# Attention, a dense MLP and routed experts in one kernel: an instruction planner that counts transfer bytes, the second batch's logits taken at once, and sums moved from TensorE to VectorE

## The chip, the cores and the metric

The kernel runs on one core of one Trainium2 chip. The metric is device time in microseconds (us); less is better. A kernel is timed in several executions, of which the median counts, and one further execution is recorded by the profiler.

## The reference, cut to what matters

```python
# q, k, v: (4 batches, 12 heads, 448, 64); w_in 768x2048, w_out 2048x768; w1 8x768x1024, w2 8x1024x768
scores = 30 * tanh((q @ k.T) / 8 / 30);  attn = softmax(scores);  x = attn @ v      # tokens 1792 x 768
h = x @ w_in;  g = h * clip(h + 3, 0, 6) / 6;  x = g @ w_out                        # dense MLP
logits = x @ w_gate                                                                 # 1792 x 8
# greedy: the largest logits first, each token to one expert, 224 tokens for each expert
out[tokens of e] = relu(x[tokens of e] @ w1[e]) @ w2[e]
```

All matrices are fp32. The dense weights come as float64 and are turned into fp32 words by integer operations on VectorE.

## The kernel before

**Three stages.** The first (to about 505 us) does attention for the four batches, the product x @ w_in with its activation g, and the logits. The second (about 505 to 797 us) does g @ w_out and, beside it, the greedy assignment in seven rounds of compares on VectorE and counts on TensorE. The third does the experts.

**The planner of the first stage.** Every step of stage one is given to `Plan.add` with an engine, a cost in us, what it reads and writes, and, for a transfer, a fixed time `land` from its issue to its landing. `Plan.run` is a list scheduler: it simulates the engines, takes at each moment the earliest step that is ready, of several the one that was added first, and emits the instructions in that order. Each engine's queue then runs in this order on the chip: an instruction that waits holds up all that stand behind it on its engine. A transfer's `land` is the same whatever else is being transferred. Names with a ring (`"ms": 1` is a single PSUM bank, `"g": 5`, `"ws": 3`, `"rb": 2`, ...) are handed on in the order of `add`.

**Attention.** A slot is half of a pair of heads (48 slots, 24 pairs, 6 pairs per batch). `score` makes two chunks of scores in PSUM, ScalarE takes tanh and exp into tiles `P`, `av` multiplies by v into `po`, and `uadd` adds the two chunks' `P` on VectorE, into `u0` for the first half of a pair and into `sb` for the second. Every second pair `fin_sum` adds over the keys: TensorE multiplies `u0` and then `sb` by ones into the bank `ms` (8 products for two pairs), VectorE makes the reciprocals `R`, SP stores them to DRAM (`rd`) and loads them back spread over the partitions (`rb`), and `fin_x` multiplies `xu` by `rb` (line 320) and splits the result into XH (a ScalarE cast, line 328, or VectorE for early pairs) and XL (line 330).

**The first product.** `m1a_pieces(b)` makes 16 column blocks f of batch b, each of 18 matmuls in three parts: wh by XH and XL for d = 0..2, the same for d = 3..5, then wl by XH for all d. Blocks f = 0, 2, 4, 6, 8 keep their split weights in SBUF (`wr`); the other 11 are split in batch 0, stored to DRAM (`wd`) and loaded again for batches 1 to 3 into the ring `ws`. From ph come r (line 540), g (line 542), and gh and gl (lines 548 and 549), which SP stores.

**Logits.** `wog_pieces` decodes w_out and multiplies it by the gate weights: transposes into `ms` (line 387), a ScalarE copy to `wot` (line 393), products (line 404). It is merged with batch 1's product. Batches 0 and 1 store g to DRAM (`gd`), and `lg_late` loads it again beside batch 2's product (line 463 multiplies). Batches 2 and 3 take their logits at once.

**Merging.** `merge` interleaves streams by their share of cost: the attention slots, the product's pieces, and what is added to them.

**The second stage.** Here the framework orders the instructions by itself. `m1b_pieces` multiplies (line 987); of w_out's blocks f = 8..15 it loads `woy`, ScalarE makes the high part `woh` (line 649), and GpSimd subtracts to the low part `wol` (line 652). The load of block f + 4 reuses a buffer of `woy` that this subtraction has read. The first eight blocks are split earlier, on ScalarE and VectorE.

Of the kernel before, what the change touches and what calls it, by code (L numbers as in the profile page):

```python
# [33 lines left out]
class Plan:  # L34
# [6 lines left out]
    HOP = 0.15  # L41

# [13 lines left out]
    def add(self, eng, cost, fn, r=(), w=(), land=0.0, after=()):  # L56
# [24 lines left out]
        deps.discard(me)  # L81
        self.ops.append((eng, cost, fn, deps, land))
        return me
# [4 lines left out]
    def run(self):  # L88
# [12 lines left out]
        total = 0.0  # L101
        for _ in range(n):
# [8 lines left out]
            _, cost, fn, _, land = self.ops[i]  # L111
            ready[eng].remove(i)
            free[eng] = t + cost
            end = t + cost + land
# [11 lines left out]
def fused_kernel(ctx: ExitStack, tc: tile.TileContext, q, k, v, cap, w_in, w_out, w_gate, w1, w2,  # L126
# [25 lines left out]
    for i in range(2):  # L152
# [7 lines left out]
    RES = [f for f in range(NF - 6) if f % 2 == 0]  # L160
# [34 lines left out]
    def load_qk(g, n):  # L195
        if g > LASTG:
            return
        b, hp = divmod(g, NP)
        key = ("t" + "kq"[n], g)
        add("SP", 0.35, lambda: nc.sync.dma_start(  # L200
            put(ap_, key, [2 * D, S]), (k, q)[n][b, 2 * hp:2 * hp + 2].rearrange("h d s -> (h d) s")), w=[key], land=2.4)

    def load_v(g):
        if g <= LASTG:
            add("SP", 0.35, lambda: nc.sync.dma_start(put(ap_, ("tv", g), [CP, 2, NC, D]), v[g // NP, g % NP]),
                w=[("tv", g)], land=2.4)
# [38 lines left out]

    def uadd(h):

        g, s_ = divmod(h, 2)
        if h < 0 or g > LASTG:
            return  # L250
        key = (("u0", "sb")[s_], g)

        def go():
            u = SB[g % 2] if s_ else put(ap_, key, [CP, 2, S])
            T[key] = u
            nc.vector.tensor_add(u[:CP], T["P", 4 * g + 2 * s_], T["P", 4 * g + 2 * s_ + 1])
        add("DVE", 1.09, go, r=[("P", 4 * g + 2 * s_), ("P", 4 * g + 2 * s_ + 1)], w=[key])
# [25 lines left out]
    def fin_sum(g):  # L283

        m, i = plan.next("ms"), g // 2

        def mm():
            p = bank(("ms", m))
            for s_ in range(2):
                for n in range(4):  # L290
                    u = T[("u0", "sb")[s_], g - 1 + n // 2]
                    r = CP + s_
                    nc.tensor.matmul(p[32 * n:32 * n + 32, :S], ones[:r], u[:r, n % 2], start=(s_ == 0), stop=(s_ == 1))  # L293
        add("PE", 1.7, mm, r=[(n, x) for n in ("u0", "sb") for x in (g - 1, g)] + [("guard", 0)], w=[("ms", m)])
# [14 lines left out]
        add("SP", 1.2, store, r=[R], w=[("RD", i)], land=2.0)  # L309
        for a in range(2):  # L310
# [4 lines left out]
            add("SP", 0.7, load, r=[("RD", i)], w=[("rb", g - 1 + a)], land=2.4)  # L315
# [32 lines left out]
    FIN = ((2, fin_sum), (4, lambda g: fin_x(g - 1)), (5, fin_x))  # L348

    def decode(src, shape, view):  # L350
# [4 lines left out]
            put(dcp, raw, shape[:-1] + [2 * shape[-1]], I32), src.bitcast(I32)), w=[raw], land=5.5)  # L355
# [14 lines left out]
    def wog_pieces():  # L370
# [3 lines left out]
        def dec(f):  # L374
            if f < NF:
                y[f] = decode(w_out[f * 128:(f + 1) * 128, :].rearrange("p (o c) -> p o c", o=1), [128, 1, DM],
                              lambda t: flat(t)[:, None, :])
                add("SP", 0.35, lambda: nc.sync.dma_start(WO[f], flat(T[y[f]])), r=[y[f]], w=[("WO", f)], land=3.0)
# [36 lines left out]
        r = [(1, lambda: (dec(0), dec(1)))]  # L415
        for f in range(NF):
            for part in range(len(PARTS)):
                r.append((300, lambda f=f, part=part: tr(f, part)))
            r.append((1, lambda f=f: dec(f + 2)))
# [12 lines left out]
    def wload(b, f):  # L432
        if f in WD:
# [6 lines left out]
            add("SP", 0.7, go, r=[("WD", f)], w=[key], land=4.0)  # L440

    def wsplit(f):
# [47 lines left out]
    def lg_late(b):  # L490
# [23 lines left out]
    def m1a_pieces(b, logits):  # L514
        gs = {}

        def mm(f, part):
# [5 lines left out]
            def go():  # L523
# [21 lines left out]
            if not logits:  # L545
                add("SP", 0.35, lambda: nc.sync.dma_start(GD[b][f], T[g]), r=[g], w=[("GD", b, f)], land=2.5)
# [31 lines left out]
    add("SP", 0.35, lambda: nc.sync.dma_start(capt, cap.to_broadcast([128, 1])), w=[("capt", 0)], land=2.0)  # L578
# [53 lines left out]
    def wo_load_p(f):  # L632
        add("SP", 0.35, lambda: wo_load(f), r=[("WO", f), ("mba", 0)], w=[("woy", f)], land=3.0)
# [556 lines left out]
```

## Time and profile before

| what | value |
|---|---|
| median of 3 runs | 1074.06 us (1073.12 to 1074.07) |
| profiled execution, its own time | 1077.6 us |
| its span, first to last instruction | 1075.6 us |
| TensorE (PE) busy | 1016.3 us, 94% |
| VectorE (DVE) busy | 732.5 us, 68% |
| ScalarE (ACT) busy | 511.1 us, 48% |
| GpSimd (POOL) busy | 150.9 us, 14% |
| bytes moved by DMA | 246.45 MB, mean 229 GB/s |

The profiled execution has 2.0 us outside its span. Busy time of PE includes matmuls that overlap, so what an idle PE costs is read from its waits and from the stretches in which it has no instruction. The granted clock is a share of 2.4 GHz: 1.00 is that level, 0.50 is 1.2 GHz.

### The profile page before, as it was taken

What the parts mean: (1) busy time and instruction counts of PE and PEld (TensorE: products, weight loads), DVE (VectorE), ACT (ScalarE), POOL (GpSimd) and SP (SyncE); (2) the same over time, 40 slices, a digit from 0 to 9 for tenths busy, and PEclk for the clock granted to TensorE, in tenths of its full rate; (3) what the DMA queues carried; (4) which work ended last, traced back from release to release, by engine and by line L of the source; (5) the groups of instructions that cost most, each with busy time, mean ns of one, the idle gap of its engine ahead of it and who ended that gap; (6) DMA issues with size and microseconds to landing.
All of it is one profiled execution on the core that took longest, in us unless ns stands there. A gap on an engine that the chain in (4) does not pass through costs nothing.

```text
span 1075.6 us, 17493 instructions
## 1 busy us (share of the span) xinstructions
PE 1016.3 (94%) x6385; PEld 829.1 (77%) x6385; DVE 732.5 (68%) x1298; ACT 511.1 (48%) x868; POOL 150.9 (14%) x154
## 2 busy tenths in 40 slices
PE   6989999699989999899899999999979999999996
PEld 2445666467666667687798899989969999999996
DVE  6898887568655444434987897778427777777673
ACT  6989877566766552433101001001116655666662
POOL 0000000000000000001500000000013555455442
PEclk8989999989999999999899999999989999999999
DMA  7467998899988669985545655537875776676760
GB/s 214 156 209 225 319 330 309 311 328 336 330 283 274 201 200 326 323 288 197 184 120 143 161 138 142 156 106 236 283 263 167 250 246 226 233 240 230 231 226 29
DMA packets 123637, 246.45 MB, mean 229 GB/s; under 512 B 23776, under 2 KB 90384, under 8 KB 123552
## 3 DMA queue, kind: packets, MB, share of 16 engines
q1 hardware_dynamic: 118960, 229.28, 64.7%
q0 software_dynamic: 3328, 11.01, 3.6%
q10 hardware_dynamic: 1264, 5.05, 1.6%
q8 instruction: 50, 0.82, 0.3%
q14 instruction: 35, 0.29, 0.1%
HBM read 182.50 MB, written 62.79 MB: 228 GB/s over the span
## 4 chain that ended last, share of the span: by engine, by line
PE 73%; DMA 12%; DVE 9%; issue 2%; ACT 2%; SPq 1%; POOL 0%; DVEq 0%; ACTq 0%; POOLq 0%
PE x L987 20%; PE py L1104 12%; PE ph L1059 7%; PE ph L533 5%; PE ph L530 5%; PE ph L531 4%; PE po L270 4%; PE ph L1061 4%; PE sc L235 3%; DMA rb<-rd 3%; PE ro L814 2%; DVE g L806 1%; PE ms L293 1%; DMA wsh<-wd 1%; DMA woy<-wo 1%
## 5 line engine op out<-in xcount | busy, mean ns | idle before, releaser
L987 PE MATMUL x<-woh,gh 128*128 128x384 f32 x448 | 127.6, 348 | 2.2 <-DMA gh<-gh 2.2
L987 PE MATMUL x<-wol,gh 128*128 128x384 f32 x448 | 124.7, 339 | 0.0
L987 PE MATMUL x<-woh,gl 128*128 128x384 f32 x448 | 123.2, 340 | 0.1
L239 ACT ACTIVATE P<-sc,rcap 112x896 f32<-112x896 f32 x96 | 92.7, 1004 | 24.1 <-PE sc L235 14.2
L530 PE MATMUL ph<-XH,wsh 128*128 128x448 f32 x264 | 99.5, 377 | 0.2 <-DVE g L542 0.2
L531 PE MATMUL ph<-XL,wsh 128*128 128x448 f32 x264 | 96.6, 366 | 0.0
L243 ACT ACTIVATE P<-P,capt 112x896 f32<-112x896 f32 x96 | 94.9, 1042 | 0.0
L270 PE MATMUL po<-P,tv 112*64 112x448 f32 x384 | 89.1, 586 | 3.4 <-ACT P L239 2.5
L987 PEld LDWEIGHTS x<-woh,gh 128*128 128x128 f32 x448 | 81.2, 191 | 9.4 <-issue 5.2
L987 PEld LDWEIGHTS x<-woh,gl 128*128 128x128 f32 x448 | 82.9, 191 | 0.7 <-DMA gl<-gl 0.4
L987 PEld LDWEIGHTS x<-wol,gh 128*128 128x128 f32 x448 | 83.2, 191 | 0.0
L540 ACT ACTIVATE r<-ph,three 128x448 f32<-128x448 f32 x64 | 40.6, 634 | 75.7 <-PE ph L533 75.7
L542 DVE SCALAR_TENSOR_TENSOR g<-r,ph 128x448 f32<-128x448 f32 x64 | 39.5, 617 | 54.1 <-ACT r L540 53.9
L806 DVE TENSOR_SCALAR g<-mrb,m 112x1344 bf16<-112x1344 f32 (+11 forms) x105 | 72.4, 701 | 0.0
L1059 PE MATMUL ph<-xe,woh 128*128 128x448 f32 x186 | 60.7, 383 | 4.5 <-DVE xe L1045 4.5
L533 PE MATMUL ph<-XH,wsl 128*128 128x448 f32 x264 | 63.4, 376 | 0.0
L530 PEld LDWEIGHTS ph<-XH,wsh 128*128 128x128 f32 x264 | 50.0, 189 | 14.3 <-issue 7.9
L722 POOL IOTA icol<- 112x112 f32 x1 | 0.2, 229 | 431.7 <-PE ph L531 431.7
L270 PEld LDWEIGHTS po<-P,tv 112*64 112x64 f32 x384 | 24.5, 144 | 46.8 <-issue 30.1
L1081 DVE SCALAR_TENSOR_TENSOR hl<-ht,hh 128x224 fp32r<-128x224 f32 x64 | 40.0, 625 | 29.3 <-ACT hh L1080 27.9
L1059 PE MATMUL ph<-xe,we 128*128 128x448 f32 x186 | 58.8, 374 | 0.0
L533 PEld LDWEIGHTS ph<-XH,wsl 128*128 128x128 f32 x264 | 49.4, 191 | 9.1 <-issue 4.4
(210 smaller groups left out, 2278.5 us busy)
## 6 DMA issues: line engine op xcount, KB each, us to landing
wol<-in_moe_w SPq DMA_DIRECT2D x32, 768.0 KB
woh<-in_moe_w SPq DMA_DIRECT2D x31, 768.0 KB
gh<-gh SPq DMA_DIRECT2D x64, 224.0 KB
gl<-gl SPq DMA_DIRECT2D x64, 224.0 KB
wsh<-wd SPq DMA_DIRECT2D x33, 384.0 KB
wsl<-wd SPq DMA_DIRECT2D x33, 384.0 KB
wraw<-in_moe_w_in SPq DMA_DIRECT2D x16, 768.0 KB
wraw<-in_moe_w_out SPq DMA_DIRECT2D x16, 768.0 KB
```

The costliest lines, as they stand in the source:

```text
L239: add("ACT", 0.96, lambda i=i: nc.scalar.activation(put(ap_, ("P", i), [CP, 2, S]), T["sc", i][:CP, :, :S], AF.Tanh, scale=rcap[:CP]), r=[ ...
L243: add("ACT", 0.99, lambda i=i: nc.scalar.activation(T["P", i], T["P", i], AF.Exp, scale=capt[:CP]), r=[("P", i), ("capt", 0)], w=[("P", i)])
L270: nc.tensor.matmul(T["po", g][64 * j:64 * j + 64, :S], T["tv", g][:, j, c, :], T["P", 4 * g + c][:, j], start=(c == 0), stop=(c == NC - 1))
L530: nc.tensor.matmul(p, wh[:, d], XH[:, d], start=(d == 0), stop=False)
L531: nc.tensor.matmul(p, wh[:, d], XL[:, d], start=False, stop=False)
L533: nc.tensor.matmul(p, wl[:, d], XH[:, d], start=False, stop=(d == KD - 1))
L540: add("ACT", 0.64, lambda: nc.scalar.activation(put(m1p, r_, [128, S]), T[key][:, :S], AF.Relu, bias=three), r=[key], w=[r_])
L806: nc.vector.tensor_scalar(g[:, s_:], mr[:, s_:], mj, None, op0=OP.is_le)
L987: nc.tensor.matmul(X2[g, i, hf][:, :HW], a, w[:, hf * HW:(hf + 1) * HW], start=bool(f == 0 and first), stop=bool(f == NF - 1 and last))
L1059: nc.tensor.matmul(p[:, :2 * TE], wh[:, d, fs], X2[:, d].rearrange("p a t -> p (a t)"), start=(d == 0), stop=False)
L1061: nc.tensor.matmul(p[:, :TE], wl[:, d, fs], X2[:, d, 0], start=False, stop=(d == KD - 1))
L1104: nc.tensor.matmul(PY[e][2 * t + hf][:CP, :384], a[:, f, tsl], w[:, f % 2, hf * 384:(hf + 1) * 384], start=bool(f == 0 and first), stop=bo ...
```

## The change

- **Planner.** A transfer now has a size `kb` in place of `land`. All transfers share one wire of 340 KB per us in order of their issue, and land 2.0 us after their last byte. The loads of `rb` are entered with 500 KB and 1.0 us of SP each (before 0.7 us of SP and 2.4 us to landing), the stores of `rd` with 8 KB, q, k, v, g, gh and gl with 224, weights with 768 or 384.
- **Weights.** Block 8 is no longer resident; the ring `g` grows from 5 to 8.
- **Sums.** For pairs 12 to 23 (batches 2 and 3) VectorE adds u0 and both chunks of the second half into `sb` (two additions in place of one), and `fin_sum` multiplies `sb` alone.
- **Order.** `fin_x` of both pairs is added one or two slots earlier; a w_out decode is added right ahead of its transposes.
- **First product.** The three parts of a block now take d = 0, 1, then 2, 3, then 4, 5, with all three products for each d, so that a part waits for two of X's blocks and not for three or all.
- **Logits.** Batches 0 and 1 are merged as one stretch; `wog_pieces` spans 37% to 89% of it. Batch 1 takes its logits at once, at blocks 6, 10 and 14 and in batch 2; its g is not stored to `gd` nor loaded again.
- **Second stage.** The subtraction to `wol` of blocks 8..15 goes from GpSimd to VectorE.

```diff
+    LAND = 2.0
+    RATE = 340.0
...
-            end = t + cost + land
+            end = t + cost
+            if kb:
+                wire = max(wire, end) + kb / self.RATE
+                end = wire + self.LAND
...
-    RES = [f for f in range(NF - 6) if f % 2 == 0]
+    RES = [f for f in range(NF - 8) if f % 2 == 0]
...
+    GB = 8
...
-                 "g": 5, "gh": 2, "gl": 2, "lacc": 1, "lacl": 1, "late": 8, "woy": 2, "gm": 4})
+                 "g": GB, "gh": 2, "gl": 2, "lacc": 1, "lacl": 1, "late": 8, "woy": 2, "gm": 4})
...
+    G3 = 12
...
-            nc.vector.tensor_add(u[:CP], T["P", 4 * g + 2 * s_], T["P", 4 * g + 2 * s_ + 1])
-        add("DVE", 1.09, go, r=[("P", 4 * g + 2 * s_), ("P", 4 * g + 2 * s_ + 1)], w=[key])
+            if s_ and g >= G3:
+                nc.vector.tensor_add(u[:CP], T["u0", g], T["P", 4 * g + 2])
+                nc.vector.tensor_add(u[:CP], u[:CP], T["P", 4 * g + 3])
+            else:
+                nc.vector.tensor_add(u[:CP], T["P", 4 * g + 2 * s_], T["P", 4 * g + 2 * s_ + 1])
+        whole = s_ and g >= G3
+        add("DVE", 2.18 if whole else 1.09, go,
+            r=[("P", 4 * g + 2 * s_), ("P", 4 * g + 2 * s_ + 1)] + [("u0", g)] * whole, w=[key])
...
+        halves = (1,) if g >= G3 else (0, 1)
...
-            for s_ in range(2):
+            for s_ in halves:
...
-        add("SP", 1.2, store, r=[R], w=[("RD", i)], land=2.0)
+        add("SP", 1.2, store, r=[R], w=[("RD", i)], kb=8)
...
-            add("SP", 0.7, load, r=[("RD", i)], w=[("rb", g - 1 + a)], land=2.4)
+            add("SP", 1.0, load, r=[("RD", i)], w=[("rb", g - 1 + a)], kb=500)
...
-    FIN = ((2, fin_sum), (4, lambda g: fin_x(g - 1)), (5, fin_x))
+    FIN = ((2, fin_sum), (3, lambda g: fin_x(g - 1)), (3, fin_x))
...
-            put(dcp, raw, shape[:-1] + [2 * shape[-1]], I32), src.bitcast(I32)), w=[raw], land=5.5)
+            put(dcp, raw, shape[:-1] + [2 * shape[-1]], I32), src.bitcast(I32)), w=[raw], kb=768)
...
-                for d in range(3 * part, 3 * part + 3) if part < 2 else ():
+                for d in range(2 * part, 2 * part + 2):
                     nc.tensor.matmul(p, wh[:, d], XH[:, d], start=(d == 0), stop=False)
                     nc.tensor.matmul(p, wh[:, d], XL[:, d], start=False, stop=False)
-                for d in range(KD) if part == 2 else ():
                     nc.tensor.matmul(p, wl[:, d], XH[:, d], start=False, stop=(d == KD - 1))
-            xs = [("X", b, n, d) for n in "hl" for d in range(3 * part, 3 * part + 3)] if part < 2 else [("X", b)]
+            xs = [("X", b, n, d) for n in "hl" for d in range(2 * part, 2 * part + 2)]
...
-                if logits and part == 1 and f % 4 == 0 and f:
+                if logits and part == 1 and f % 4 == logits - 1 and f > 3:
...
+    WO0, WO1, AP = 0.7, 0.2, 0.1
...
-    for b in range(1, B):
-        body, end = m1a_pieces(b - 1, b - 1 >= 2)
-        body.insert(int(len(body) * 0.9), (0, lambda b=b: (wload(b, 0), wload(b, 1))))
-        extra = wog_pieces() if b == 2 else lg_late(0) + lg_late(1) if b == 3 else []
-        merge(A[cut[b]:cut[b + 1]], body, extra)
-        if b == 2:
-            add("none", 0.0, turn_dec, w=[("room", 0)], after=plan.using({"wraw", "wy", "wot"}))
+    def m1a(b, logits):
+        body, end = m1a_pieces(b, logits)
+        body.insert(int(len(body) * 0.9), (0, lambda: (wload(b + 1, 0), wload(b + 1, 1))))
+        return body, end
+
+    def pad(stream, share):
+        return [(share * sum(c for c, _ in stream), lambda: None)]
+
+    body, end = m1a(1, 3)
+    extra = wog_pieces()
+    merge(A[cut[1]:cut[3]], m1a(0, 0)[0] + body, pad(extra, WO0) + extra + pad(extra, WO1))
+    add("none", 0.0, turn_dec, w=[("room", 0)], after=plan.using({"wraw", "wy", "wot"}))
+    body, end2 = m1a(2, 1)
+    body = body[:4] + end + body[4:]
+    end = end2
+    merge(A[cut[3]:] + pad(A[cut[3]:], AP), body, lg_late(0))
...
-                    wo_split(f + 2, mb, nc.gpsimd)
+                    wo_split(f + 2, mb, nc.vector)
```

## Rows read from the trace of the kernel before

**Rows 1.** Windows: length; busy PE, PEld, DVE, ACT, POOL; granted clock; DMA share, GB/s.

```profile
100.00:192.00 92.00, 91.69 (x521) 63.87 (x520) 75.97 (x113) 74.62 (x106) 0.00 (x0) 1.00 0.92 317
192.00:331.00 139.00, 124.42 (x867) 89.00 (x866) 84.75 (x130) 88.00 (x138) 0.00 (x0) 0.95 0.90 314
331.00:431.00 100.00, 98.00 (x537) 65.95 (x537) 46.68 (x76) 47.87 (x69) 0.00 (x0) 1.00 0.76 248
431.00:505.00 74.00, 69.24 (x345) 55.08 (x343) 31.48 (x50) 27.20 (x44) 2.02 (x13) 1.00 0.81 279
505.00:545.00 40.00, 33.85 (x234) 29.58 (x235) 38.28 (x61) 6.09 (x10) 17.14 (x8) 0.91 0.52 162
545.00:775.00 230.00, 229.42 (x1697) 210.44 (x1697) 180.14 (x440) 20.55 (x46) 0.65 (x1) 1.00 0.57 164
```

**Rows 2.** Waits of PE, 192 to 331 us: total, times, longest.

```profile
PE ms L387 <- ACT wot L393: 11.9, 3, 8.4
PE ms L387 <- DVE wog L411: 1.6, 1, 1.6
```

**Rows 3.** Timelines of PE, DVE, 196 to 222 us: start, length, instruction, [idle].

```profile
214.34 0.90 PE L387 MATMUL ms<-ident,wy 128*128 128x128 f32 x3 [8.42 <-ACT wot L393]
...
204.86 0.63 DVE L320 TENSOR_TENSOR xu<-xu,rb 128x448 f32<-128x448 f32 x1 [6.67 <-DMA rb<-rd]
...
212.14 0.63 DVE L320 TENSOR_TENSOR xu<-xu,rb 128x448 f32<-128x448 f32 x1 [5.12 <-DMA rb<-rd]
```

**Rows 4.** SP's timeline at 194 us, then two pieces of the chain.

```profile
194.51 3.48 SPq L308 DMA_DIRECT2D rd<-R  x4
...
155.56 7.12 DMA wraw<-in_moe_w_out
...
294.31 7.75 DMA rb<-rd
```

**Rows 5.** Windows behind the two longest waits of PE, columns as in rows 1.

```profile
214.30:219.20 4.90, 4.86 (x15) 2.11 (x16) 3.53 (x6) 3.26 (x5) 0.00 (x0) 0.50 1.02 347
305.80:309.20 3.40, 3.38 (x11) 3.08 (x12) 2.70 (x4) 3.40 (x4) 0.00 (x0) 0.51 0.49 180
```

**Rows 6.** Chain, one fin_sum; additions into sb: ns min/median/max, first and last.

```profile
119.15 1.64 PE ms L293 x16
...
L256 DVE TENSOR_TENSOR sb<-P x24: 1078/1083/1093, 19.3 to 389.2; 112x896 f32<-112x896 f32 x24
```

**Rows 7.** Waits of PE for late logits, 331 to 431, 431 to 505 us.

```profile
PE ms L463 <- DMA gl<-gd: 2.0, 2, 1.4
...
PE ms L463 <- DMA gl<-gd: 2.7, 1, 2.7
```

**Rows 8.** First block of batch 0 by line, 60 to 100 us; window 60 to 90 us.

```profile
L530 PE MATMUL ph<-XH,wrh x6: 362/367/471, 64.1 to 89.1; 128*128 128x448 f32 x6
...
60.00:90.00 30.00, 26.81 (x156) 13.49 (x154) 27.30 (x42) 26.84 (x34) 0.00 (x0) 0.88 0.72 230
```

**Rows 9.** Waits of PE and of ACT, 505 to 545 us.

```profile
PE ro L814 <- DVE g L806: 4.7, 3, 2.2
...
ACT woh L649 <- DMA woy<-wo: 16.7, 5, 6.3
```

**Rows 10.** Line 652 by engine: ns min/median/max, first and last start.

```profile
L652 DVE TENSOR_TENSOR wol<-woy,woh x8: 957/958/959, 427.5 to 456.6; 128x768 fp32r<-128x768 f32 x8
L652 POOL TENSOR_TENSOR wol<-woy,woh x8: 1832/2108/3172, 504.6 to 533.2; 128x768 fp32r<-128x768 f32 x8
```

**Rows 11.** DVE by form, 505 to 545 us; the same, 545 to 579 us.

```profile
L806 DVE TENSOR_SCALAR g<-mrb,m 112x1344 bf16<-112x1344 f32 x4 | 6.6, 1696 | 0.0
...
L795 DVE TENSOR_TENSOR eqd<-eqd,upto 112x1344 bf16<-112x1344 bf16 x1 | 2.5, 2472 | 0.0
...
L806 DVE TENSOR_SCALAR g<-mrb,m 112x1344 bf16<-112x1344 f32 x4 | 3.5, 920 | 0.0
...
L795 DVE TENSOR_TENSOR eqd<-eqd,upto 112x1344 bf16<-112x1344 bf16 x1 | 0.9, 857 | 0.0
```

More of the change, by code (lines that the diff above doesn't have):

```diff
@@ L54, in next, with add @@
         return n
-    def add(self, eng, cost, fn, r=(), w=(), land=0.0, after=()):
+    def add(self, eng, cost, fn, r=(), w=(), kb=0, after=()):
         me = len(self.ops)
@@ L81, in add @@
         deps.discard(me)
-        self.ops.append((eng, cost, fn, deps, land))
+        self.ops.append((eng, cost, fn, deps, kb))
         return me
@@ L100, in run @@
         free = {}
-        total = 0.0
+        total = wire = 0.0
         for _ in range(n):
@@ L110, in run @@
             t, i, eng = best
-            _, cost, fn, _, land = self.ops[i]
+            _, cost, fn, _, kb = self.ops[i]
             ready[eng].remove(i)
             free[eng] = t + cost
-            end = t + cost + land
+            end = t + cost
+            if kb:
+                wire = max(wire, end) + kb / self.RATE
+                end = wire + self.LAND
             total = max(total, end)
@@ L200, in load_qk @@
         add("SP", 0.35, lambda: nc.sync.dma_start(
-            put(ap_, key, [2 * D, S]), (k, q)[n][b, 2 * hp:2 * hp + 2].rearrange("h d s -> (h d) s")), w=[key], land=2.4)
+            put(ap_, key, [2 * D, S]), (k, q)[n][b, 2 * hp:2 * hp + 2].rearrange("h d s -> (h d) s")), w=[key], kb=224)
     def load_v(g):
@@ L205, in load_v @@
             add("SP", 0.35, lambda: nc.sync.dma_start(put(ap_, ("tv", g), [CP, 2, NC, D]), v[g // NP, g % NP]),
-                w=[("tv", g)], land=2.4)
+                w=[("tv", g)], kb=224)
     def split(g, n):
@@ L292, in mm @@
                     r = CP + s_
-                    nc.tensor.matmul(p[32 * n:32 * n + 32, :S], ones[:r], u[:r, n % 2], start=(s_ == 0), stop=(s_ == 1))
-        add("PE", 1.7, mm, r=[(n, x) for n in ("u0", "sb") for x in (g - 1, g)] + [("guard", 0)], w=[("ms", m)])
+                    nc.tensor.matmul(p[32 * n:32 * n + 32, :S], ones[:r], u[:r, n % 2], start=(s_ == halves[0]), stop=(s_ == 1))
+        add("PE", 0.85 * len(halves), mm, r=[(("u0", "sb")[n], x) for n in halves for x in (g - 1, g)] + [("guard", 0)], w=[("ms", m)])
         t, R = ("R", 2 * i), ("R", 2 * i + 1)
@@ L374, in dec @@
         def dec(f):
[L375 to L378, printed above, removed]
+            y[f] = decode(w_out[f * 128:(f + 1) * 128, :].rearrange("p (o c) -> p o c", o=1), [128, 1, DM],
+                          lambda t: flat(t)[:, None, :])
+            add("SP", 0.35, lambda: nc.sync.dma_start(WO[f], flat(T[y[f]])), r=[y[f]], w=[("WO", f)], kb=384)
         def tr(f, part):
+            if part == 0:
+                dec(f)
             m, q_, i = plan.next("ms"), f // 4, f % 4
@@ L413, in mm @@
                 r=[("ms", m2)], w=[("wog", q_)])
-        r = [(1, lambda: (dec(0), dec(1)))]
+        r = []
         for f in range(NF):
@@ L439, in go @@
                     nc.sync.dma_start(T[key][i].bitcast(F32), WD[f][i])
-            add("SP", 0.7, go, r=[("WD", f)], w=[key], land=4.0)
+            add("SP", 0.7, go, r=[("WD", f)], w=[key], kb=768)
     def wsplit(f):
@@ L454, in wsplit @@
             add("SP", 0.7, lambda: [nc.sync.dma_start(WD[f][i], T[key][i].bitcast(F32)) for i in range(2)],
-                r=[key], w=[("WD", f)], land=3.0)
+                r=[key], w=[("WD", f)], kb=768)
     def lg_mm(b, tiles, first, pool):
@@ L498, in go @@
                 add("SP", 0.35, lambda f=f, key=key: nc.sync.dma_start(put(lp(), key, [128, S], name="gl"), GD[b][f]),
-                    r=[("GD", b, f), ("room", 0)], w=[key], land=2.6)
+                    r=[("GD", b, f), ("room", 0)], w=[key], kb=224)
                 st[f4].append((f, key))
@@ L545, in mm @@
             if not logits:
-                add("SP", 0.35, lambda: nc.sync.dma_start(GD[b][f], T[g]), r=[g], w=[("GD", b, f)], land=2.5)
+                add("SP", 0.35, lambda: nc.sync.dma_start(GD[b][f], T[g]), r=[g], w=[("GD", b, f)], kb=224)
             hi, lo = ("gh", n), ("gl", n)
@@ L552, in mm @@
                 add("SP", 0.35, lambda i=i, x=x: nc.sync.dma_start(GHL[b][f][i], T[x].bitcast(F32)),
-                    r=[x], w=[("GHL", b, f, i)], land=2.5)
+                    r=[x], w=[("GHL", b, f, i)], kb=224)
         def lg(f4):
@@ L577, in fused_kernel @@
     nc.gpsimd.memset(wgt, 0.0)
-    add("SP", 0.35, lambda: nc.sync.dma_start(capt, cap.to_broadcast([128, 1])), w=[("capt", 0)], land=2.0)
+    add("SP", 0.35, lambda: nc.sync.dma_start(capt, cap.to_broadcast([128, 1])), w=[("capt", 0)], kb=1)
     def rate():
@@ L593, in fused_kernel @@
     add("DVE", 1.6, guards, r=[("gexp", 0)], w=[("guard", 0)])
-    add("SP", 0.35, lambda: nc.sync.dma_start(wgt[:, :, 0:E], w_gate), w=[("wgt", 0)], land=2.5)
+    add("SP", 0.35, lambda: nc.sync.dma_start(wgt[:, :, 0:E], w_gate), w=[("wgt", 0)], kb=24)
     A = [(3200, lambda h=h: slot(h)) for h in range(NH + 6)]
     LAG = 6
+    WO0, WO1, AP = 0.7, 0.2, 0.1
     nb = 2 * NP
@@ L632, in wo_load_p @@
     def wo_load_p(f):
-        add("SP", 0.35, lambda: wo_load(f), r=[("WO", f), ("mba", 0)], w=[("woy", f)], land=3.0)
+        add("SP", 0.35, lambda: wo_load(f), r=[("WO", f), ("mba", 0)], w=[("woy", f)], kb=384)
     def wo_split_p(f):
@@ L683, in g_load @@
             GS[n] = ts
-    body, end2 = m1a_pieces(B - 1, True)
-    body = body[:2] + end + body[2:] + end2
+    body, end2 = m1a_pieces(B - 1, 1)
+    body = body[:4] + end + body[4:] + end2
     def first_loads():
         for n in range(3):
-            add("SP", 0.7, lambda n=n: g_load(n), r=[("GHL", 0, n, 0), ("GHL", 0, n, 1), ("mba", 0)], w=[("gm", n)], land=2.5)
+            add("SP", 0.7, lambda n=n: g_load(n), r=[("GHL", 0, n, 0), ("GHL", 0, n, 1), ("mba", 0)], w=[("gm", n)], kb=400)
     body.insert(int(len(body) * 0.9), (0, first_loads))
```

1 line of the change is left out of this document (removed).

## The prediction

> **What bounds the kernel now.** I read the windows by stage first, because the share of busy time over the whole span hides which stage has time to give. In [rows 1] PE is busy for 99.7% of 100 to 192 us and of 545 to 775 us: there only less PE work makes the end earlier. From 192 to 331 us, the stretch of batch 1's product, it is idle for 14.6 of 139 us and the granted clock averages 0.95. From 331 to 505 us it is idle for 6.8 us, from 505 to 545 us for 6.2 us at a clock of 0.91. DVE is the nearest rival only from 505 to 545 us, where it is busy for 38.3 of 40 us.
>
> Then the waits of PE. Between 192 and 331 us 11.9 us are a wait for the ScalarE copy to `wot`, and 1.6 us for `wog` [rows 2]. The name is not the cause. The timeline [rows 3] shows PE idle for 8.4 us until 214.3 us, and in the same stretch DVE standing twice, 6.7 and 5.1 us, before the multiplication of `xu` by `rb`, for the transfer of `rb`. The ScalarE cast of X waits for that multiplication, the copy to `wot` stands behind the cast in ScalarE's queue, and the single bank `ms` keeps PE waiting. The chain shows the same transfer of `rb` with 7.75 us at 294 us [rows 4], ahead of the other waits. The planner before counts 2.4 us to its landing. In the first case it is 17.6 us from the first store of `rd` at 194.5 us to the multiplication at 212.1 us [rows 3, 4], where the plan has 1.2 + 2.0 + 2 times 0.7 + 2.4 = 7.0 us. The queue of transfers is what the plan doesn't know: DMA is at 0.90 to 0.92 of its share from 100 to 331 us [rows 1], and a w_out load of 768 KB took 7.1 us [rows 4].
>
> **The change part by part.** The sum is made against the profiled execution's own 1077.6 us (a span of 1075.6 us and 2.0 us outside); the median of the runs is 0.9967 of it.
>
> *Sums on VectorE.* A `fin_sum` of 16 recorded matmuls takes 1.64 us of PE [rows 6]. Half of them, 0.82 us, go in each of the six of pairs 12 to 23: -4.9 us of PE, all in stretches where PE is the bound. VectorE gets 12 additions of 1.08 us [rows 6], 13.0 us, where it is busy for 85 of 139 and 47 of 100 us [rows 1]: hidden. Without this cover it would cost up to 13 us, and it keeps two tiles `P` 1.1 us longer, which delays the next tanh; ScalarE is at 48% from 331 us on.
>
> *Planner by bytes.* `rb` is now planned with 1.0 us of SP each and 500/340 + 2.0 = 3.5 us to landing, behind whatever is on the wire. So the multiplication comes later in DVE's queue, and what stood behind it (decodes, g, the split of K) goes first. At stake: 11.9 + 1.6 = 13.5 us of idle PE [rows 2], and behind the two long waits 4.9 and 3.4 us at a granted clock of 0.50 (the 1.2 GHz level), after PE had been idle; half of those 8.3 us is lost, 4.2 us [rows 5]. Together 17.7 us. Below nothing would need a new wait (rival 2 below), so the bounds are 0 and 17.7. I take 13: the plan's 7.0 us become about 9.2 us (1.2 + 2.0 + 2.0 + 1.5 + 1.5 + 1.0), plus the queue that it now counts, and 17.6 us were needed, so the remedy is large but not whole.
>
> *Weights of the gate earlier.* The 16 decodes are the same work. Their loads already begin at 155.6 us in batch 0's product [rows 4], since the planner takes whatever is ready; what moves is the rank of the transposes in the `ms` ring. Nothing by itself; in cover of this stands DVE, 61% busy. SP's queue gets for block 8 one pair of stores and three pairs of loads of 768 KB more, and loses 16 stores and 16 loads of 224 KB.
>
> *Logits of batch 1 at once.* The four products stay. The waits for late loads are 2.0 and 2.7 us [rows 7]; the load before the later one is batch 1's, which is gone, and half as many loads compete. I take 4 of 4.7; the bounds are 0 and 4.7.
>
> *Three equal parts.* Before, the first block of batch 0 has 3 of its 6 matmuls with XH at 64 us and the other 3 only at 89 us [rows 8], since part two needs blocks 3 to 5 of X. Now 24 matmuls of the first two blocks, not 12, can run when four of X's blocks are there. From 60 to 90 us PE is idle for 3.2 us [rows 8], which caps this: I take 2, bounds 0 and 3.2.
>
> *`wol` on VectorE.* Added to DVE: 8 x 0.958 us = 7.7 us [rows 10], in the one stretch where DVE is nearly full [rows 1]. Removed: GpSimd's eight subtractions of about 2.1 us. While they run, DVE's compares are long: the form of 1344 elements takes 1.70 us against 0.92 us later, the product of ties 2.47 against 0.86 us [rows 11], together 4 x 0.78 + 1.6 = 4.7 us. If each of the eight cost 1.6 us like the tie product, it would be 12.9 us. I take 9 us between them, so DVE is 1.3 us better off (bounds -3.0 and +5.2). PE waits for those compares for 4.7 us [rows 9], and a mean clock of 0.91 over 40 us is 7.2 us at the lower level, 3.6 us lost [rows 1]. I take 2 us of the at most 8.3.
>
> The Trainium skill, "SBUF — State Buffer", section "Who interferes with whom", has it that such a VectorE instruction and a GpSimd instruction exclude each other for a whole instruction. By that, an estimate, 8 x 2.1 = 16.9 us of DVE would come free, PE's 4.7 us would go entirely, and the sum would be 2.7 us better; the rows above show less per instruction.
>
> **The sum.** 4.9 + 13 + 4 + 2 + 2 = 25.9 us; 1077.6 - 25.9 = 1051.7 us; times 0.9967 it is 1048 us.
>
> **The rivals.**
>
> *Rival 1: the wait for `rb` stays or moves*, and the planner's part does nothing; this is also the case in which the change doesn't do what it says. For it: DMA's share in the stretch hardly falls (a saving of 16 x 0.23 MB of stores against some 1.6 MB more for block 8), and q, k and v stand in the same queue. Against it: DVE has other work that it could do meanwhile. 1077.6 - 12.9 = 1064.7, or 1061 us.
>
> *Rival 2: VectorE's queue waits for w_out's transfers.* Where: 505 to 545 us. `wol` needs `woh`, and ScalarE waits 16.7 us for `woy` in that stretch [rows 9]; so far only ScalarE and GpSimd stood, now the compares stand behind `wol`, and behind them PE's counts; SP's loads of `woy` wait for `wol` too, and the loads of gh and gl behind these. If DVE stood for all of it: 16.7 + 7.7 - 9 = +15.4 in place of -2: 1077.6 - 23.9 + 15.4 = 1069.1, or 1066 us. For it: DVE has 1.7 us to spare there. Against it: TensorE needs block 8 only half-way through, and the framework may place the subtractions late.
> The same follows from the Trainium skill, "TensorE: Matmul & The Clock Gate", section "Architectural detail: the array is 16× 32×32, not 1× 128×128": VectorE and ScalarE take their queues strictly in order. The trace agrees where `xu` holds up DVE for 6.7 us [rows 3].
>
> *Rival 3: slower, by transfers in batch 1's product.* The w_out loads get a higher rank than before while block 8 is streamed too. Each 768 KB ahead of a streamed pair costs 0.79 MB / 317 GB/s = 2.5 us [rows 1]; if all 12 pairs of batch 1 met one, +30 us, with the 17.7 us not recovered: 1077.6 - 12.9 + 30 = 1094.7, or 1091 us. It decides from six of the 12 on (12.9 / 2.5 = 5.2). Against it: no wait of PE for a streamed weight is among those of 192 to 331 us [rows 2], and 0.90 leaves a tenth.
>
> **How the numbers follow.** The forecast has a chance of 0.64, rival 1 0.20, rival 2 0.09, rival 3 0.07. A difference below 0.2% (2.1 us) can't be told from none. All of the forecast, nearly all of rival 1 and most of rival 2 lie beyond it on the fast side: faster 0.88; 0.03 within; slower 0.09 (rival 3, and 0.02 of rival 2 with less recovered elsewhere). All upper bounds give 4.9 + 17.7 + 4.7 + 3.2 + 8.3 = 38.8 us, 1035 us; the upper end takes in rivals 1 and 2: 1066 us. Rival 3 and small remainders stay outside.
>
> **What would show it.** Right: no wait of PE above 3 us between 192 and 331 us, DVE's waits before `xu` far below 6 us, `fin_sum` of late pairs at 8 matmuls and about 0.8 us, no `gd` loads of batch 1, block 0 of batch 0 finished well before 89 us, compares of 0.9 us in the first routing round, and the first stage ending some 24 us before 505 us. Wrong: DVE idle for `woh` at the start of the second stage; waits of PE for `ws` in batch 1's product; a long `rb` wait elsewhere, with the clock at 0.50 behind it.

## The result and the profile after

The changed kernel takes 1040.36 us (median of 4 runs, 1037.31 to 1042.89) against 1074.07 us before: a ratio of 0.968, 95% interval 0.965 to 0.972, 3.2% faster. The forecast was 1048 us, in a range of 1035 to 1066 us. The profiled span falls from 1075.6 to 1041.1 us. Read from the first matmuls of the stages in both traces, the first stage ends at 475.6 us and not 505.4 (-29.8 us), the second takes 290.2 us and not 295.3 (-5.1 us), the third is unchanged (266.9 us to the last product, before 266.5).

Windows of the changed kernel, cut where its stages are; columns as in [rows 1], to which they answer:

```profile
100.00:188.00 88.00, 88.00 (x497) 61.66 (x496) 73.69 (x106) 73.12 (x106) 0.00 (x0) 1.00 0.93 327
188.00:314.00 126.00, 122.88 (x862) 86.19 (x861) 93.37 (x141) 87.27 (x134) 0.00 (x0) 0.99 0.93 325
314.00:405.70 91.70, 91.70 (x506) 64.63 (x505) 48.89 (x78) 48.39 (x70) 0.00 (x0) 1.00 0.73 236
405.70:475.60 69.90, 67.06 (x336) 54.72 (x335) 30.42 (x47) 27.34 (x43) 1.56 (x12) 1.00 0.89 308
475.60:515.60 40.00, 38.29 (x279) 34.67 (x278) 34.96 (x82) 4.72 (x7) 0.00 (x0) 1.00 0.56 162
515.60:740.60 225.00, 223.26 (x1651) 203.30 (x1649) 178.71 (x429) 21.59 (x47) 0.99 (x1) 1.00 0.59 167
```

Batch 1's product (second row) now leaves PE idle for 3.1 us in place of 14.6, at a clock of 0.99. What PE waits for there, 188 to 314 us, is this (before: [rows 2]):

```profile
PE ms L403 <- DVE wy L378: 2.2, 1, 2.2
PE ms L403 <- DVE lacc L487: 0.7, 1, 0.7
PE ms L403 <- ACT wot L409: 0.2, 1, 0.2
```

The view of the tile `rb` before and in the changed kernel (what its readers' engine waited for, total, times); two of the 14 waits of before are in [rows 3]:

```profile
L320 DVE TENSOR_TENSOR xu<-xu,rb x24: 611/625/629, 42.4 to 416.7; 128x448 f32<-128x448 f32 x24
its engine sat idle before it (us, times) until:
  DMA rb<-rd: 38.4, 14
```
```profile
L335 DVE TENSOR_TENSOR xu<-xu,rb x24: 614/619/626, 39.9 to 392.8; 128x448 f32<-128x448 f32 x24
its engine sat idle before it (us, times) until:
  DMA rb<-rd: 3.8, 4
```

A late `fin_sum` in the chain has 8 matmuls, and the last waits of PE from 314 us to the end of the first stage are small; no late load is among them (before: [rows 6, 7]):

```profile
374.92 0.89 PE ms L308 x8
```
```profile
PE ph L545 <- DMA wsh<-wd: 1.2, 1, 1.2
PE ms L497 <- DVE lacc L487: 0.9, 1, 0.9
PE ms L478 <- DVE g L556: 0.6, 1, 0.6
PE ph L547 <- DMA wsl<-wd: 0.2, 1, 0.2
```

In the second stage the tie product (line 819) is short from the start, and `wol` stands among VectorE's groups (475 to 512 us, by form; before: [rows 11]). Its wait for `woh`, 0.7 us, is the whole of rival 2:

```profile
L676 DVE TENSOR_TENSOR wol<-woy,woh 128x768 fp32r<-128x768 f32 x5 | 4.7, 954 | 0.7 <-ACT woh L673 0.7
L830 DVE TENSOR_SCALAR g<-mrb,m 112x1344 bf16<-112x1344 f32 x4 | 3.5, 912 | 0.0
...
L819 DVE TENSOR_TENSOR eqd<-eqd,upto 112x1344 bf16<-112x1344 bf16 x1 | 0.8, 850 | 0.0
```

Only batch 0's stored g is loaded again, 16 loads (before, 32):

```profile
L513 SPq DMA_DIRECT2D gl<-gd x16: 319/432/1653, 302.8 to 361.6; - x16
```

All marks that the prediction set for its right case are there; the first stage ends 29.8 us earlier, where it had some 24. That doesn't say which part earned the 34 us. The experiments do, and there the prediction's sum fares worse than its total.

### The profile page after: what moved, and what is told of

The parts are those of the page before. It is cut to its first block, busy times and chain, and to the rows that moved or that the text cites. A ratio compares the mean times of both kernels' runs of the same rounds, so it can differ in the third digit from the quotient of the medians.

```text
span 1041.1 us, 17395 instructions
## 1 busy us (share of the span) xinstructions
PE 1000.4 (96%) x6337; PEld 821.4 (79%) x6337; DVE 740.9 (71%) x1318; ACT 510.9 (49%) x868; POOL 132.6 (13%) x146
## 4 chain that ended last, share of the span: by engine, by line
PE 79%; DMA 9%; DVE 8%; ACT 2%; issue 1%; SPq 0%; POOL 0%; ACTq 0%; POOLq 0%; DVEq 0%
PE x L1011 18%; PE py L1128 13%; PE ph L1083 8%; PE ph L545 7%; PE ph L547 7%; PE ph L546 7%; PE po L284 5%; PE sc L241 4%; PE ph L1085 4%; PE ro L838 2%; DMA wraw<-in_moe_w_out 2%; DMA gh<-gh 1%; PE ms L478 1%; DMA mrb<-md 1%; DMA wsl<-wd 1%
## 5 line engine op out<-in xcount | busy, mean ns | idle before, releaser
L545 PE MATMUL ph<-XH,wsh 128*128 128x448 f32 x288 | 111.1, 386 | 1.2 <-DMA wsh<-wd 1.2
L547 PE MATMUL ph<-XH,wsl 128*128 128x448 f32 x288 | 106.0, 368 | 0.2 <-DMA wsl<-wd 0.2
L546 PE MATMUL ph<-XL,wsh 128*128 128x448 f32 x288 | 105.8, 367 | 0.0
L284 PE MATMUL po<-P,tv 112*64 112x448 f32 x384 | 85.2, 566 | 5.9 <-ACT P L245 3.2
L545 PEld LDWEIGHTS ph<-XH,wsh 128*128 128x128 f32 x288 | 54.4, 189 | 26.8 <-issue 16.9
L830 DVE TENSOR_SCALAR g<-mrb,m 112x1344 bf16<-112x1344 f32 (+11 forms) x105 | 68.1, 660 | 0.0
L547 PEld LDWEIGHTS ph<-XH,wsl 128*128 128x128 f32 x288 | 54.2, 188 | 5.8 <-DMA wsl<-wd 0.8
L546 PEld LDWEIGHTS ph<-XL,wsh 128*128 128x128 f32 x288 | 54.4, 189 | 3.9
```

The lines of the kernel that those rows point to most:

```text
L284: nc.tensor.matmul(T["po", g][64 * j:64 * j + 64, :S], T["tv", g][:, j, c, :], T["P", 4 * g + c][:, j], start=(c == 0), stop=(c == NC - 1))
L830: nc.vector.tensor_scalar(g[:, s_:], mr[:, s_:], mj, None, op0=OP.is_le)
```

## The experiments

Each run was timed beside the kernel before; its ratio to it is compared with the changed kernel's 0.968 (0.965 to 0.972). The ends of the four products of stage one are the last matmuls of each batch in the trace of the profiled execution, which is one execution for each kernel.

| run | median us | ratio to before, 95% interval | products of batches 0 to 3 end at us | stage one ends | stage two takes |
|---|---|---|---|---|---|
| before | 1074.07 | 1 | 192.2, 331.6, 430.8, 501.7 | 505.4 | 295.3 |
| changed kernel | 1040.36 | 0.968 (0.965 to 0.972) | 188.0, 314.0, 405.7, 472.0 | 475.6 | 290.2 |
| fixed times again | 1076.13 | 1.000 (0.997 to 1.002) | 209.1, 344.5, 438.2, 504.1 | 507.7 | 293.9 |
| before, rb at 8 us | 1064.09 | 0.989 (0.984 to 0.993) | 193.6, 319.1, 419.9, 489.7 | 493.3 | 293.8 |
| wire, rb small | 1041.98 | 0.968 (0.964 to 0.972) | 188.6, 313.2, 405.5, 470.1 | 473.8 | 292.8 |
| wol on GpSimd | 1044.80 | 0.970 (0.967 to 0.973) | 188.5, 312.2, 403.9, 468.8 | 472.5 | 296.0 |
| no VectorE sums | 1042.47 | 0.968 (0.966 to 0.970) | 188.2, 315.5, 408.1, 473.2 | 476.9 | 290.0 |
| old parts | 1048.06 | 0.972 (0.971 to 0.974) | 191.1, 320.2, 411.8, 475.9 | 479.6 | 291.0 |
| late logits of batch 1 | 1075.17 | 0.998 (0.996 to 1.000) | 189.2, 312.2, 412.0, 505.0 | 508.6 | 291.1 |
| fixed times, rb at 8 us | 1056.73 | 0.980 (0.977 to 0.982) | 199.8, 325.6, 417.3, 484.2 | 487.8 | 293.2 |
| planner alone | 1067.31 | 0.991 (0.987 to 0.994) | 186.8, 303.0, 423.6, 489.3 | 493.3 | 294.7 |
| gate weights in batch 1 | 1040.80 | 0.965 (0.961 to 0.969) | 187.0, 306.4, 403.7, 468.9 | 472.8 | 291.3 |
| late logits, block 8 resident | 1070.11 | 0.991 (0.988 to 0.995) | 191.9, 303.0, 432.6, 498.5 | 502.2 | 290.8 |
| wire at 300 | 1064.55 | 0.987 (0.983 to 0.991) | 191.9, 329.7, 424.9, 493.2 | 496.8 | 290.2 |

Two traces of one program differ too, and the table shows by how much. Stage one of the run with `wol` on GpSimd has the changed kernel's instructions in the same order, and ends at 472.5 us and not at 475.6: 3.1 us. Stage two has the same instructions in the same order in the ten programs that have these subtractions on VectorE; it takes 290.0 to 293.9 us (mean 291.5). In the four that have them on GpSimd it takes 293.8 to 296.0 us (mean 294.9). So a difference of 3 us in one stage is not told from none by two traces.

### Fixed times again

```diff
-    LAND = 2.0
-    RATE = 340.0
+    FIX = {1: 2.0, 8: 2.0, 24: 2.5, 224: 2.5, 384: 3.0, 400: 2.5, 500: 2.4, 768: 4.0}
...
-                wire = max(wire, end) + kb / self.RATE
-                end = wire + self.LAND
+                end += self.FIX[kb]
...
-            add("SP", 1.0, load, r=[("RD", i)], w=[("rb", g - 1 + a)], kb=500)
+            add("SP", 0.7, load, r=[("RD", i)], w=[("rb", g - 1 + a)], kb=500)
```

> The changed kernel, but the planner again gives each transfer a fixed time to landing (rb 2.4 us and 0.7 us of SP, 224 KB 2.5, 384 KB 3.0, 768 KB 4.0 us) and knows no shared wire; all else of the change stays. Theory (planned transfer times took away the stalls behind rb): VectorE's waits for rb come back, 15 us or more in total against 3.8 us, and the time is 12 to 18 us above the changed kernel's 1040: 1052 to 1058 us. Rival (the gain comes from the equal parts, the merging and the logits, not from the transfer times): at most 3 us above it, 1040 to 1043 us.

The whole gain is gone, more than the theory's 12 to 18 us; the rival falls. VectorE's wait for `rb` and, behind it, PE's for `wot` are back (waits of DVE, then of PE, 20 or 60 to 510 us):

```profile
DVE xu L333 <- DMA rb<-rd: 41.3, 18, 7.6
```
```profile
PE ms L401 <- ACT wot L407: 10.2, 2, 8.1
PE ms L423 <- DVE wot L422: 4.7, 1, 4.7
PE ph L543 <- DVE g L554: 3.1, 1, 3.1
```

All other parts of the change together, without the planner, end the first stage 2.3 us later than before, so they gain nothing. They even move the stall: batch 0's product ends at 209.1 us, 16.9 us later than before, and the longest wait for `wot` falls into it, where the kernel before has none (waits of PE, 20 to 209 us):

```profile
PE ms L401 <- ACT wot L407: 8.1, 1, 8.1
```

The fixed times are not quite the old ones: a decoded block's load of 768 KB had 5.5 us before and has 4.0 us here. What that adds was not tried.

### Before, rb at 8 us

```diff
-            add("SP", 0.7, load, r=[("RD", i)], w=[("rb", g - 1 + a)], land=2.4)
+            add("SP", 0.7, load, r=[("RD", i)], w=[("rb", g - 1 + a)], land=8.0)
```

> The kernel before, with one figure changed: the planner's time to landing of an rb load is 8.0 us in place of 2.4. Theory (rb's figure alone was the fault): VectorE's waits for rb fall from 38.4 us to under 10 us, the 8.4 us wait of TensorE goes, and the time falls by 10 to 17 us to 1057 to 1064 us. Rival (all transfers have to be counted on one wire, since other late transfers then take rb's place): within 3 us of 1074 us, with new waits for q, k, v or w_out of the same size.

The theory holds. One number in the plan of the old kernel is worth 1.1%: the first stage ends 12.1 us earlier, and VectorE's waits for `rb` fall to 1.8 us. PE's waits for the ScalarE copy to `wot` fall from 11.9 us to 0.8 us. That is the mechanism of [rows 2, 3], shown by itself, and about the 13 us that the prediction gave to the planner.

```profile
DVE xu L320 <- DMA rb<-rd: 1.8, 3, 0.7
```
```profile
PE ms L387 <- ACT wot L393: 0.8, 1, 0.8
```

### Wire, rb small

```diff
-            add("SP", 1.0, load, r=[("RD", i)], w=[("rb", g - 1 + a)], kb=500)
+            add("SP", 0.7, load, r=[("RD", i)], w=[("rb", g - 1 + a)], kb=112)
```

> The changed kernel, but an rb load is entered with 112 KB and 0.7 us of SP in place of 500 KB and 1.0 us; the shared wire stays. Theory that rb's own figure matters: VectorE waits for rb 12 us or more in total and the time rises by 6 us or more, to 1046 us or above. Rival (the wire, which counts what stands ahead of rb, does it by itself): waits for rb under 8 us, and within 3 us of 1040 us.

The time is the changed kernel's, as the rival had it; but VectorE waits 16.9 us for `rb` in 14 waits, as the theory had it. Both are half right: with the wire, most of these waits are no longer on PE's path. The inflated 500 KB are not what the time needs.

### Fixed times, rb at 8 us

The edit of the first experiment with 8.0 us for an `rb` load.

> The changed kernel without the shared wire: fixed times as in the first experiment (224 KB 2.5, 384 KB 3.0, 768 KB 4.0 us), but rb lands after 8.0 us. Theory that rb's figure alone is needed: within 4 us of 1040 us. Theory that the wire is needed for the other transfers too (q, k, v, w_out, ws): rb's waits vanish but 10 us or more remain, 1050 to 1062 us, with waits of VectorE and ScalarE for wraw, tk, tq of 10 us or more.

`rb`'s figure gives back 19.9 of the 32.1 us by which stage one with fixed times lies behind the changed kernel's (507.7 to 487.8 us); the other 12.2 us come with the wire. Whether they need a shared queue, or only longer fixed times for the other transfers, isn't shown: 4.0 us stand here for 768 KB, where [rows 4] has 7.1 us, and longer ones were not tried. VectorE and PE no longer wait for `rb`; ScalarE's cast of Q waits 7.7 us for `tq`, and VectorE 10.0 us for w_out, in waits of up to 6.7 us:

```profile
ACT QH L220 <- DMA tq<-in_q: 7.7, 2, 6.7
```

### Planner alone

```diff
-            end = t + cost + land
+            end = t + cost
+            if kb:
+                wire = max(wire, end) + kb / self.RATE
+                end = wire + self.LAND
```

with the change's sizes for every transfer, in the kernel before.

> The kernel before with the new planner alone: sizes and the shared wire with the figures of the change, nothing else of it. Theory (counting transfers is enough by itself, the other parts add little): first stage 487 us or less, total 1050 to 1058 us. Rival (the planner gains only together with the logits taken at once, since late logits put their loads into batches 2 and 3): first stage 495 us or more, total 1064 to 1078 us, waits for late loads of 8 us or more.

The rival holds for the total. Stage one, 493.3 us, lies between the theory's 487 and the rival's 495 us, and the waits for late loads are 7.1 us, not 8. The table shows where the time goes: batch 1's product ends at 303.0 us, 28.6 us ahead of before and ahead of the changed kernel too; then batch 2's product needs 120.6 us in place of 99.2 and gives 21.4 of them back. A small part of this is work that only moved: 48 of the 192 products with `wot` now run after batch 1's end, before none. Most of it is a stretch at the end of batch 2's product, with 36 matmuls in 23.6 us at a mean clock of 0.64. Waits of PE, the 48 products' window, then that stretch:

```profile
PE ms L468 <- DMA gl<-gd: 7.1, 4, 3.7
```
```profile
303.00:423.60 120.60, 1.52 (x48) 1.25 (x48) 0.93 0.79 265
400.00:423.60 23.60, 14.24 (x36) 6.57 (x36) 9.95 (x14) 6.21 (x9) 0.00 (x0) 0.64 0.93 311
```

### Late logits of batch 1

```diff
-    body, end = m1a(1, 3)
+    body, end = m1a(1, 0)
...
-    merge(A[cut[3]:] + pad(A[cut[3]:], AP), body, lg_late(0))
+    merge(A[cut[3]:] + pad(A[cut[3]:], AP), body, lg_late(0) + lg_late(1))
```

> The changed kernel, but batch 1 stores g and takes its logits late, beside batch 2's product after those of batch 0. Theory: the waits for late logits come back, 4 us in the last two batches, and DMA carries 7.3 MB more; total 1043 to 1046 us. Rival (with transfers planned, late logits are hidden): within 2 us of 1040 us.

The whole gain is gone again: 33 us in the first stage, where 4 us were predicted and 3 to 6 expected here. Until batch 1's end the run is as fast as the changed kernel; batch 2's product takes 99.8 us in place of 91.7 and batch 3's 93.0 in place of 66.3. Timeline of PE, then a window, of that run:

```profile
424.27 1.70 PE L478 MATMUL ms<-gl,wog 128*32 128x448 f32 x2 [4.85 <-DMA gl<-gd]
427.84 0.74 PE L545 MATMUL ph<-XH,wrh 128*128 128x448 f32 x1 [0.44 <-ACT XH L343]
439.12 1.70 PE L478 MATMUL ms<-gl,wog 128*32 128x448 f32 x2 [6.36 <-DMA gl<-gd]
```
```profile
424.00:449.00 25.00, 15.94 (x42) 8.34 (x43) 9.87 (x14) 6.74 (x10) 1.56 (x12) 0.57 0.71 234
```

After the first wait the clock is at 1.2 GHz for most of the time until 449 us (0.57 on the mean), and batch 3's first product waits for a cast of X. The last product of `fin_sum` comes at 406 us, 29.5 us after the last one of attention (376.5 us); in the changed kernel it is 7.0 us (367.9 and 374.9 us). The code says why it can: late products and `fin_sum` share the bank `ms` in the order of `add`, so the last pairs' sums stand behind late products that wait for their loads, and batch 3's X behind the sums. The chain of this run (start, length) shows the end of it once, from a late load of 6.9 us to batch 3's product:

```profile
417.29 6.94 DMA gl<-gd
424.27 1.72 PE ms L478 x2
...
426.55 0.63 DVE xu L335
427.21 0.58 ACT XH L343
427.84 0.74 PE ph L545
```

This order was not changed by itself; that it costs the 33 us is argued.

### Late logits, block 8 resident

The edit above, and

```diff
-    RES = [f for f in range(NF - 8) if f % 2 == 0]
+    RES = [f for f in range(NF - 6) if f % 2 == 0]
...
-    GB = 8
+    GB = 5
```

> The changed kernel with batch 1's logits late, and block 8 resident and a ring of five g as before. Theory (the 33 us that late logits cost came of transfers: 12 streamed blocks and 32 loads together pass what DMA carries beside batch 2): taking 0.79 MB per batch away gives most back, 1045 to 1058 us. Rival (their place in the order does it: batch 3's first matmuls stand behind the last late products): 1066 to 1078 us, with waits for gd loads of 8 us or more before batch 3.

The rival's 1070 us: fewer bytes give back only 6 us of stage one. Batch 2's product takes 129.6 us here, and PE waits 8.9 us for late loads. The last sum is again 29 us behind attention (363 and 392 us). Batch 3's product takes 65.9 us, as in the changed kernel: here the late products stand, with their waits, ahead of the end of batch 2's product.

```profile
405.00:432.60 27.60, 16.67 (x41) 6.19 (x40) 12.16 (x17) 7.64 (x11) 0.00 (x0) 0.63 0.94 313
```

All three runs that take batch 1's logits late under the new planner have such a stretch: 36 to 42 matmuls in 24 to 28 us, at a clock of 0.57 to 0.64. At the pace of the changed kernel's fourth window (336 in 69.9 us) they would take 7.5 to 9 us, an estimate, so 16 to 19 us are lost in it each time. So block 8's transfers are not what makes late logits dear. The place of the late products in the order is the likely cause; that their loads come late for another reason isn't excluded, since loads of `gd`, `woy` and gh share SP's queue there and no run moved one of them alone.

### Wire at 300

```diff
-    RATE = 340.0
+    RATE = 300.0
```

> The changed kernel with the planner's wire at 300 KB per us in place of 340, nearer to the 229 to 337 GB/s of its stages. Theory (the plan needs a queue, not its exact rate): within 3 us of 1040 us, either way. Rival (the rate is critical): 1046 us or more, or 1034 us or less.

The theory falls: 21 us more in the first stage, 15.7 of them by the end of batch 1's product. That stretch moves 289 GB/s at a DMA share of 0.85 and leaves PE idle for 12.7 us, in many small waits, of which none stands behind `rb`:

```profile
191.90:329.70 137.80, 125.08 (x833) 84.98 (x833) 93.74 (x141) 82.20 (x127) 0.00 (x0) 0.95 0.85 289
```

The rival, that the rate is critical, holds. The likely reason is that a plan for a wire slower than the real one (325 GB/s here in the changed kernel) orders the engines' work by it, and each engine's queue then keeps that order. Only two rates were tried; whether 340 is the best, and how much of the 21 us is mere chance of the order, stays open.

### The small parts

```diff
-                    wo_split(f + 2, mb, nc.vector)
+                    wo_split(f + 2, mb, nc.gpsimd)
```

> The changed kernel, but the eight subtractions to wol in the second stage are on GpSimd again. Theory (the second stage's gain of 5.1 us, 295.3 to 290.2 us from its first matmul to the first of the experts, is VectorE freed of the blocked compares): the stage takes 294 to 296 us and the total is 4 to 6 us above the changed kernel's, 1044 to 1046 us, with compares of 1344 elements of 1.6 us or more again. Rival (the stage gained because its first transfers now start under less load): the stage stays at 290 to 291.5 us and the total at 1040 to 1042 us.

The theory holds. The second stage is 296.0 us, with PE's waits for compares back (4.8 us), the tie product at 2.47 us and the clock at 0.91 for its first 40 us. The total rises by less, 2 to 4 us, since stage one of this trace ended 3.1 us earlier by chance. By-form groups of VectorE, 472 to 512 us, and the first 40 us, of this run; then the whole second stage of this run and of the changed kernel:

```profile
L830 DVE TENSOR_SCALAR g<-mrb,m 112x1344 bf16<-112x1344 f32 x4 | 6.6, 1695 | 0.0
...
L819 DVE TENSOR_TENSOR eqd<-eqd,upto 112x1344 bf16<-112x1344 bf16 x1 | 2.5, 2466 | 0.0
```
```profile
472.50:512.50 40.00, 33.90 (x234) 29.99 (x233) 38.27 (x61) 6.32 (x9) 15.46 (x8) 0.91 0.51 158
472.50:768.40 295.90, 281.86 (x2021) 256.58 (x2019) 223.73 (x510) 30.43 (x62) 18.14 (x11) 0.98 0.59 175
```
```profile
475.60:765.90 290.30, 280.25 (x2023) 255.06 (x2021) 218.90 (x519) 30.24 (x62) 2.29 (x3) 0.99 0.61 179
```

VectorE is busy for 4.8 us less in the changed kernel (218.9 against 223.7), although it does the eight subtractions there, 7.6 us of work: 12.4 us come free.

Without the VectorE sums:

```diff
-    G3 = 12
+    G3 = 24
```

> The changed kernel, with the four-chunk sums taken back: every fin_sum multiplies u0 and sb again, VectorE does two additions a pair. Theory (TensorE is the bound from 100 us to the end of the first stage, so its work counts one for one): 6 x 0.82 = 4.9 us more, first stage 480.5 us against 475.6, total 1044 to 1047 us. Rival (VectorE's 13 us of additions cost part of it): total 1040 to 1043 us, with less VectorE work in batches 2 and 3.

The ratio is the changed kernel's, the first stage 1.3 us longer. The rival's total holds: the saving of PE is there (a `fin_sum` takes 0.89 us for 1.64), but what arrives of it can't be told from none.

With the old three parts of a block:

```diff
-                for d in range(2 * part, 2 * part + 2):
+                for d in range(3 * part, 3 * part + 3) if part < 2 else ():
...
+                for d in range(KD) if part == 2 else ():
                     nc.tensor.matmul(p, wl[:, d], XH[:, d], start=False, stop=(d == KD - 1))
...
```

> The changed kernel with the three parts of a block as before (d = 0..2, d = 3..5, then wl over all d). Theory: the first block of batch 0 ends at 85 us or later against 64.2 us, the first stage takes 2 to 3 us more, total 1042 to 1044 us. Rival (attention fills TensorE there anyway, nothing follows): total within 2 us of 1040 us.

4.0 us more in stage one, 4 to 8 us in total: more than expected. Block 0's last part starts at 84.6 us, not at 62.7. The products of batches 0 and 1 take 3 us more each, which would fit a coarser wait that costs again at the change of batch; this is argued.

With the gate weights merged into batch 1 alone:

```diff
-    merge(A[cut[1]:cut[3]], m1a(0, 0)[0] + body, pad(extra, WO0) + extra + pad(extra, WO1))
+    merge(A[cut[1]:cut[2]], m1a(0, 0)[0])
+    merge(A[cut[2]:cut[3]], body, extra + pad(extra, WO1))
```

> The changed kernel with the gate weights merged into batch 1's product alone again, from its start. Theory (their earlier rank is worth nothing by itself): within 4 us of 1040 us. Rival (the early start clears the bank ms and the transfers for the logits of batch 1): 1048 us or more, with waits for wog or wot before the logits of batch 1.

No difference that can be told; their early start earns nothing here.

No run beats the changed kernel beyond its interval.

## Why the prediction was right in total and wrong in its sum

**What bounds the kernel: right.** The wait for `wot` was one for `rb`: raising `rb`'s figure alone removes it and 12 us.

**Planner, 13 of at most 17.7 us: right for the planner alone, which takes 12.1 us off the first stage.** With the other parts in place its loss costs 32 us (fixed times again, where a decoded block's load has a shorter time than before, too). What failed is that it was summed as a term by itself: the bound came from the waits of the old order, and the other parts make a new order, in which with fixed times the wait for `wot` stands in batch 0's product already.

**Logits at once, 4 of at most 4.7 us: the step that failed most.** It was sized by the waits for late loads [rows 7]. With everything else in place it is worth 33 us. The prediction asked what the late loads delay now, and not what they would delay once batch 1 ended earlier. By the code the late products can only start when w_out is done, and they stand in the same bank as the last sums, for which batch 3 waits. The runs with late logits show what it comes to: 7 to 12 us of waits for `gd`, and a stretch in which waits and low clock together lose some 16 to 19 us. Where the rest of the 33 us goes stays open.

**The parts don't add.** The first stage ends earlier than before by -2.3 us with all but the planner, by -3.2 us with all but batch 1's logits at once (508.6 us), by 12.1 us with the planner alone, and by 29.8 us with all. A sum of terms, each read from the same old trace, could only come out near by luck: the 13 and the 4 stand for two parts of which neither has its whole gain without the other. The two of them alone, without the small parts, were not run.

**Sums on VectorE, 4.9 us: too large**, at most 2 us seen, which can't be told from none. The duration was nearly right, 0.75 us saved for each `fin_sum` and not 0.82. "All in stretches where PE is the bound" was the wrong step: before, three of the six sums concerned (48 products of line 293) run between 192 and 331 us, where [rows 1] has PE idle for 14.6 us. Why so little arrives where PE is nearly always busy stays open. (ScalarE, put at 48% "from 331 us on", is at 48% until 431 us and at 37% after it [rows 1]; nothing hangs on it.)

**Three parts, 2 of at most 3.2 us: too small**, 4 us; only batch 0's start had been counted.

**Gate weights earlier, nothing: right.**

**`wol`, 2 of at most 8.3 us: right in kind**, 3.5 us on the mean of all traces; the 5.1 us between the two kernels are in part chance. VectorE is free of the long forms, and PE's waits for compares fall from 4.7 to 0.8 us. The step on VectorE was too small: 9 us were to come free, 12.4 do, so VectorE is 4.8 us better off and not 1.3. The rule of the Trainium skill, "SBUF — State Buffer", section "Who interferes with whom", that such a VectorE instruction and a GpSimd instruction exclude each other for a whole instruction, came nearer. The trace agrees with it in the main: GpSimd's eight subtractions take 15.5 us in the run that has them, and 12.4 us of VectorE's time go with them.

**Rivals.** Rival 1 is gone: 38.4 us of waits for `rb` became 3.8. Rival 2 is gone: VectorE waited 0.7 us. Rival 3 needed waits for streamed weights in batch 1; there are none, and 1.4 us later.

## What to carry to other kernels

A static order is only as good as its picture of a shared resource that is nearly full, here DMA at 0.90 to 0.92 of its share. Give a planner the sizes of its transfers and one queue for them, near the rate that the trace shows, and look at who stands behind a late transfer rather than at the engine that the wait names. By itself that was worth no more here than one honest figure for the worst transfer, 12.1 us each.

When a stall is removed, ask which chain becomes next with the time saved, not only how long the visible waits are: here two edits cost 32 and 33 us when they are taken back, and of the first, alone, only 12 us are seen. Undo each part from the finished version and also try it alone; the two answers differ where parts depend on each other. And before a few us are read out of one trace, look at how far two traces of the same program differ.

## What the runs showed of the hardware that was not expected

Behind two waits of PE of 4.9 and 6.4 us, 15 us apart, the granted clock was 0.57 on the mean for 25 us (late logits of batch 1). PE was busy for 15.9 us of them; at 2.4 GHz, an estimate, the same work would have taken some 7 us less, which the clock cost beside the 11.2 us of the waits. Beside GpSimd's subtractions of 2.0 us a VectorE compare of 112x112 took 1.83 us (`wol` on GpSimd), in the changed kernel 0.27 us:

```profile
L828 DVE TENSOR_SCALAR g<-mrb,m 112x112 bf16<-112x112 f32 x1 | 1.8, 1833 | 0.0
```
```profile
L828 DVE TENSOR_SCALAR g<-mrb,m 112x112 bf16<-112x112 f32 x1 | 0.3, 270 | 0.0
```

And the 16 DMA engines carried 345 GB/s of mixed reads and writes at a share of 1.00 over 130 us of the planner-alone run, against 314 GB/s at 0.90 over batch 1's product in the kernel before [rows 1].

```profile
190.00:320.00 130.00, 130.00 (x912) 95.08 (x916) 84.75 (x130) 89.43 (x140) 0.00 (x0) 1.00 1.00 345
```
